# More unused matmuls in an attention kernel's opening, and one more unit whose exponentials are added on VectorE

## The chip, the cores and the metric

The kernel runs on one core of a Trainium2 chip. The metric is device time in microseconds (us) of one execution of the whole program. Engines are named as in the profile: PE (TensorE matmul), PEld (its weight load), DVE (VectorE), ACT (ScalarE), POOL (GpSimd) and SP (SyncE, which issues DMAs).

## What is computed

Attention with normalized queries and keys, followed by a two-layer network with a leaky ReLU:

```python
def rmsnorm(x, g):
    return x / np.sqrt(np.mean(x * x, axis=-1, keepdims=True) + 1e-06) * g

def _attn_ref(q, k, v, g_q, g_k):          # q, k, v: 8 x 12 x 448 x 64, float32
    q_n, k_n = (rmsnorm(q, g_q), rmsnorm(k, g_k))
    scores = (1.0 / np.sqrt(64)) * np.matmul(q_n, k_n.transpose(0, 1, 3, 2))
    scores = scores - np.max(scores, axis=-1, keepdims=True)
    attn = np.exp(scores)
    attn = attn / (np.sum(attn, axis=-1, keepdims=True) + 1e-09)
    return np.matmul(attn, v)

def _moe_ref(x, w_in, w_out):               # x: 3584 x 768, w_in: 768 x 2048, w_out: 2048 x 768
    h = x @ w_in
    g = np.maximum(0.01 * h, h)
    return g @ w_out
```

`x` is the attention's output with the twelve heads of a token side by side.

## The kernel before

**Units.** The 96 heads (8 batches of 12) are worked in 24 units of four heads (`u` from 0 to 23; batch `u // 3`). A unit's scores come in seven steps `t`, one for each group of 64 keys per head. `qk` (line 202, with the matmuls in line 199) writes one step's scores into a PSUM slot of two banks (there are two such slots); `ex` (line 209, instruction in line 218) lets ACT take the exponential of it into the tile `et[t]`, 128x896 in 16 bits. Softmax needs one shift for a unit: `shift_max` (line 225) lets DVE take the maximum of the first step (line 236) and put it on a diagonal (line 238); `shift_mm` (line 243) spreads it over the partitions with a small matmul (line 248 in the loop, line 254 in the opening), and DVE makes the bias `eb` of it (lines 249 and 255 to 257). All exponentials of the unit wait for `eb`.

**Sums and values.** When unit `u + 1` has begun, PE multiplies the values of unit `u` (`pv_slot`, line 364) and sums its exponentials. In the units called narrow (4 to 22) the sums come from `zcol` (line 299, matmuls in line 307): four matmuls of 32 columns for each tile of a list that `z_tiles` (line 294) gives. The list is all seven `et[t]`, or, for a unit named in the table `ADDED`, the last ones and one tile `ea` that holds the sum of the first `ADDED[u]`. DVE makes `ea` in `add_e` (line 288, instructions in line 292), with one addition fewer than there are tiles in it. ACT then takes the reciprocal by a logarithm and an exponential (`zcol_ln`, `zcol_inv`), and four DMAs on SP's queue spread it into `rz` (line 334). ACT copies the values' product to `x32` (line 319), and `xmul_sb` on DVE or `xmul_pool` on POOL multiplies both into the network's input `xt` (line 344).

**The network.** Each batch's first layer is 16 groups of six matmuls (`moe1`, line 386) with the ReLU on ACT (line 380); the second layer is taken for pairs of batches, partly by a product with seven multiplications instead of eight (`seven`), for which DVE makes sums of blocks (lines 449 to 458) and puts the results together (line 475). These pieces wait in `queue` with a cost each, and `fill` (line 726) takes as many of them as fall due after each of a unit's four stages `d` (stage 0 has step 0, stages 1 to 3 have two steps each). After each piece one of the `jobs` of the stage is called; what is left of the jobs comes at the end of the stage. The order in which instructions are written is the order in which each engine works: the schedule is made by hand.

**The loop around unit 7.** In stage 2 of a unit that has four or more added tiles, `add_e(u)` and then `xmul_sb(u - 1)` are called directly after the exponentials, ahead of the jobs. In units 6 and 7 before, which have no entry in `ADDED`, `xmul_sb(u - 1)` is the last job of stage 2, behind the normalization of unit `u + 2` (`prep_rinv` on ACT, `prep_norm` in line 171 on DVE, and a transposing DMA, `prep_trd`).

**The opening.** Units 0 to 2 are written out step by step (lines 769 to 949). For unit 0, `prep_norm` makes normalized q and k in 16 bits, in chunks; PE transposes them (`tr`, line 801), ACT and DVE copy the result into `qkT` (lines 752, 756, 758), and the scores follow. `warm(n, bank)` (line 764) issues `n` matmuls of a 128x128 tile of ones with itself, into columns of a bank that nobody reads. Before there are eight such places: 32 and 42 ahead of unit 0's transposes, then 6, 12, 8, 10, 8 and 12 in the opening of units 0 to 2. The single banks come from a ring of four (`aux`).

Of the kernel before, what the change touches and what calls it, by code (L numbers as in the profile page):

```python
# [18 lines left out]
def kernel(  # L19
# [37 lines left out]
    def aux(shape, dtype, name):  # L57
        if held:
            return held[0].pop(0)
        return psum.tile(shape, dtype, tag="aux", bufs=4, name=name)  # L60
# [51 lines left out]
    st = {}  # L112
# [25 lines left out]
    def buf(u, name):  # L138
        if name not in st[u]:
            shape, dtype, bufs = SHAPES[name]  # L140
            st[u][name] = prep_p.tile(shape, dtype, tag=name[:2] if bufs == 3 and name != "qkT" else name, bufs=bufs, name=name)
        return st[u][name]
# [3 lines left out]
    def prep_sq(u, c=ALL, tis=BOTH):  # L146
        for ti in tis:
            nc.scalar.activation(buf(u, f"sq{ti}")[:, :, c[0]:c[1]], raw[u][ti][:, :, c[0]:c[1]], AF.Square)  # L148
# [44 lines left out]
    def slot():  # L193
        return psum.tile([P, 2, 512], FP32, tag="sT", bufs=2, name="sT")

    def score(u, t, banks):
        for r in range(2):
            for a in range(2):
                nc.tensor.matmul(banks[a][64 * r:64 * r + 64, 0:S].rearrange("p (t x) -> p t x", t=NS),  # L199
                                 kT(u, r, a, t), qT(u, r, a), start=True, stop=True)  # L200

    def qk(u, steps):
        st[u]["sT"] = []
        for t in steps:
            sT = slot()
            score(u, t, (sT[:, 0], sT[:, 1]))
            st[u]["sT"].append((t, sT))

    def ex(u):
        s = st[u]  # L210
        if "et" not in s:
            s["et"] = epool.tile([P, NS, 2, S], FP16, tag="et", name="et")
        for t, sT in s["sT"]:
            if isinstance(sT, list):
                for a in range(2):
                    nc.scalar.activation(s["et"][:, t, a], sT[a][:, 0:S], AF.Exp, bias=s["eb"], scale=1.0)
            else:
                nc.scalar.activation(s["et"][:, t], sT[:, :, 0:S], AF.Exp, bias=s["eb"], scale=1.0)  # L218
# [21 lines left out]
    def shift_bank(u):  # L240
        st[u]["pb"] = aux([P, 512], FP32, "pb")
# [39 lines left out]
                                     e[64 * r:64 * r + 64, a], start=(i == 0), stop=(i == len(ets) - 1))  # L281

    HS = S // 2
    ADDED = {u: 4 for u in (10, 11, 13, 16, 17, 19)}
    ADDED.update({3: 5, 4: 5, NU - 1: 5})
    ADDED.update({u: 3 for u in (8, 14, 20, 22)})

    def add_e(u):
        s = st[u]
        s["ea"] = zpool.tile([P, 2, S], FP16, tag="ea", name="ea")  # L290
        for t in range(1, ADDED[u]):
            nc.vector.tensor_tensor(s["ea"], s["et"][:, 0] if t == 1 else s["ea"], s["et"][:, t], op=ALU.add)  # L292

    def z_tiles(u):
        s = st[u]
        ets = [s["et"][:, t] for t in range(NS)]
        return ets[ADDED[u]:] + [s["ea"]] if "ea" in s else ets

# [465 lines left out]
    def warm(n, bank):  # L764
        for x in range(n):
            nc.tensor.matmul(bank[:, P:2 * P], onesp, onesp, start=True, stop=True)

    with tc.manual_schedule():
# [7 lines left out]
        wbank = aux([P, 512], FP32, "warm")  # L776
# [1 line left out]
        for a in range(2):  # L778
            nc.vector.scalar_tensor_tensor(gdup[:, a], grow[:, 0], 0.125, grow[:, 1], op0=ALU.mult, op1=ALU.mult)
        nc.tensor.matmul(gps[:, 0:1], gdup.rearrange("o a d -> o (a d)"), one32, start=True, stop=True)  # L780
        warm(42, wbank)
        prep_sq(0, CA, (0,))
        prep_sq(0, CB, (0,))
        prep_sq(0, ALL, (1,))
# [11 lines left out]
        def tr(u, ti, chunks, tp=None):  # L796
            if tp is None:
                tp = aux([P, NS, P], FP16, "tp")
            for c, copy in chunks:
                for x in range(*c):  # L800
                    nc.tensor.transpose(tp[:, x, :], buf(u, "n16")[:, ti, x].rearrange("p a d -> p (a d)"), ident16)
                copy(buf(u, "qkT")[:, ti, c[0]:c[1]], tp[:, c[0]:c[1]], ti == 0)
            return tp

        tr(0, 0, ((CA, acopy),))
        tr(0, 0, ((CB, acopy),))
        tpk = tr(0, 1, ((K0, vcopy),))
        prep_sq(1, ALL, (0,))
        qk(0, STEPS[0])
        shift_max(0)  # L810
# [7 lines left out]
        load_v(1)  # L818
        load_v(2)
        shift_bank(0)  # L820
        warm(6, st[0]["pb"])
        shift_mm(0)
        prep_ssq(1)

# [56 lines left out]
        for f in range(2):  # L881
            load_w_out(8 * f, 8)
        qk(1, (2,))
        ex(1)
        trn(2, 0, vcopy)
        qk(1, (3,))
# [27 lines left out]
        prep_sqp(5)  # L914
        load_v(5)
        qk(2, (2,))
        ex(2)
        trn(3, 0, vcopy)
        trn(3, 1, vcopy)
# [31 lines left out]
        for u in range(3, NU):  # L951
            for d in range(4):
                if d > 0 or u > 3:
                    qk(u, STEPS[d])
                    if d == 0:
                        shift_max(u)
                        if u == 6:
                            xmul_sb(u - 2)
                        if narrow(u - 1):
                            pv_slot(u - 1)  # L960
                            zcol(u - 1)
                            shift_mm(u)
                            pv_out(u - 1)
                        else:
                            zsum_slot(u - 1)
                            pv(u - 1)
                            shift_mm(u)
                            zinv(u - 1)
                    ex(u)
                    if d == 0 and narrow(u - 1):  # L970
                        zcol_ln(u - 1)
                if d == 2 and ADDED.get(u, 0) > 3 and u < NU - 1:
                    add_e(u)
                    if u > 4:
                        xmul_sb(u - 1)
                jobs = []

                def job(fn, *args):
                    jobs.append(lambda: fn(*args))

                if d == 0:
                    if u == 3:
                        prep_norm(4)
                        gate(4)
                    elif narrow(u - 1):
                        if u < NU - 1:
                            job(zcol_inv, u - 1)
                    else:
                        xmul(u - 1)
                    if u + 4 < NU:  # L990
                        job(load, u + 4)
                    if u + 3 < NU:
                        load_v(u + 3)
                    if u < 6:
                        prep_sqp(u + 3)
                if d == 1 and narrow(u - 1) and not 5 <= u < 8 and ADDED.get(u, 0) < 4:
                    xmul_pool(u - 1)
                if u == NU - 1:
                    if d == 1:
                        job(zcol_inv, u - 1)  # L1000
                if fed(u, d) and u > 3:
                    push(u // NQ - 1)
                if (u, d) in ((3, 1), (4, 0)):
                    for ti in range(2):
                        prep_tr(u + 1, ti, VV)
                if d == 1 and 5 <= u < NU - 1:
                    job(prep_g, u + 1)
                if u + 2 < NU:
                    if d == 1:
                        if ADDED.get(u) == 3:  # L1010
                            job(lambda u: (prep_ssq(u + 2), add_e(u)), u)
                        else:
                            for ti in range(2):
                                job(prep_ssq, u + 2, ALL, (ti,))
                    if d == 2:
                        job(prep_rinv, u + 2)
                        for ti in range(2):
                            job(prep_norm, u + 2, ALL, (ti,))
                        if u > 3:
                            job(prep_trd, u + 2)  # L1020
                if d == 1 and 4 <= u < 8:
                    job(weight_sum, u - 4, 0)
                if d == 0 and 5 <= u < 9:
                    job(weight_sum, u - 5, 1)
                if d == 2 and 6 <= u < 8:
                    job(xmul_sb, u - 1)
                if d == 1 and u == NU - 2:
                    jobs.append(lambda: None)
                    job(add_e, u)
                if u == NU - 2 and d == 0:  # L1030
                    for n, tile_ in ((1, (raws, "rq", 3)), (2, (raws, "rk", 3)), (3, None), (4, (prep_p, "sq", 3))):
                        job(win_sum, n, 1, tile_)
                    for n in (3, 1, 2, 4):
                        job(x_sum, LATE, n)
                if u == NU - 1 and d == 3:
                    job(add_e, u)
                    job(xmul_sb, u - 1)
                if d == 3 and 6 <= u < NU - 3:
                    for ti in range(2):
                        job(prep_sq, u + 3, ALL, (ti,))  # L1040
                fill(u, d, jobs)
# [39 lines left out]
```

## Time and profile before

| what | value |
|---|---|
| median of four timed runs | 418.12 us (418.05 to 418.16) |
| profiled execution, its own time | 417.42 us |
| its span, first to last instruction | 415.6 us |
| mean granted TensorE clock in it | 0.999 |
| PE busy | 398.5 us, 96% of the span |
| DVE busy | 302.0 us, 73% |
| ACT busy | 303.6 us, 73% |
| POOL busy | 68.8 us, 17% |
| DMA | 62.41 MB, mean 150 GB/s |

How to read it: times are from the span's start. A row of the timeline gives the start, the time until the last of the row's instructions ends, engine, line, operation, what is written from what with its shape, and how many instructions; the bracket is the engine's idle time before it and who ended it. The chain view is the work that ended last, followed backwards: at each step what released the instruction, or the one before it on its engine. Matmuls overlap: one alone takes longer than the distance from one to the next in a row of them. The page's second part has one digit for each fortieth of the span, the busy share in tenths.

### The profile page before, as it was taken

What the parts mean: (1) busy time and instruction counts of PE and PEld (TensorE: products, weight loads), DVE (VectorE), ACT (ScalarE), POOL (GpSimd) and SP (SyncE); (2) the same over time, 40 slices, a digit from 0 to 9 for tenths busy, and PEclk for the clock granted to TensorE, in tenths of its full rate; (3) what the DMA queues carried; (4) which work ended last, traced back from release to release, by engine and by line L of the source; (5) the groups of instructions that cost most, each with busy time, mean ns of one, the idle gap of its engine ahead of it and who ended that gap; (6) DMA issues with size and microseconds to landing.
All of it is one profiled execution on the core that took longest, in us unless ns stands there. A gap on an engine that the chain in (4) does not pass through costs nothing.

```text
span 415.6 us, 9315 instructions
## 1 busy us (share of the span) xinstructions
PE 398.5 (96%) x3807; PEld 218.6 (53%) x3807; DVE 302.0 (73%) x485; ACT 303.6 (73%) x474; POOL 68.8 (17%) x70
## 2 busy tenths in 40 slices
PE   8787999999999999999999999999999999999995
PEld 7454444544445544455445544455445557558863
DVE  5888897986688756866668756867669788557762
ACT  6998888678887699867987689867985657653600
POOL 1867432200010200020020100020002202000000
PEclk9999999999999999999999999999999999999999
DMA  6999998889666995678664996788552460033023
GB/s 212 264 258 250 240 247 160 200 162 208 148 155 88 219 241 101 152 180 176 155 156 70 221 204 127 147 175 183 158 99 45 121 158 9 9 76 77 2 56 97
DMA packets 71950, 62.41 MB, mean 150 GB/s; under 512 B 36324, under 2 KB 67044, under 8 KB 71908
## 3 DMA queue, kind: packets, MB, share of 16 engines
q1 hardware_dynamic: 61312, 49.62, 47.8%
q0 software_dynamic: 10272, 11.80, 18.1%
q8 instruction: 30, 0.49, 0.5%
q10 hardware_dynamic: 324, 0.39, 0.3%
q14 instruction: 12, 0.10, 0.1%
HBM read 45.61 MB, written 11.01 MB: 136 GB/s over the span
## 4 chain that ended last, share of the span: by engine, by line
PE 78%; DVE 9%; ACT 8%; issue 3%; DMA 1%; SPq 0%; DVEq 0%; ACTq 0%
PE hps L386 27%; PE sT L199 8%; PE sT L364 5%; PE ma L468 5%; PE md L468 5%; ACT et L218 5%; PE mc L468 5%; PE bank L588 4%; PE bank L468 4%; PE op L427 4%; PE mb L468 2%; DVE n L171 2%; PE zc L307 2%; PE sT L468 2%; DVE sT L236 1%
## 5 line engine op out<-in xcount | busy, mean ns | idle before, releaser
L218 ACT ACTIVATE et<-sT,eb 128x896 f16<-128x896 f32 x166 | 159.5, 1011 | 18.8 <-PE sT L199 17.0
L386 PE MATMUL hps<-xt,win 128*128 128x448 f16 x600 | 120.8, 353 | 0.2 <-DVE xt L373 0.2
L386 PEld LDWEIGHTS <-win 128*128 128x128 f16 x612 | 56.8, 98 | 58.1 <-issue 9.7
L380 ACT ACTIVATE gt<-hps 128x448 f16<-128x448 f32 x100 | 54.0, 556 | 6.1 <-PE hps L386 5.3
L199 PE MATMUL sT<-qkT 64*64 64x448 f16 x664 | 52.4, 363 | 4.4 <-ACT et L218 3.4
L159 DVE TENSOR_REDUCE ssq<-sq 128x14 f32<-128x896 f32 (+2 forms) x49 | 50.1, 1058 | 0.4 <-ACT sq L148 0.4
L468 PEld LDWEIGHTS <-sa 128*128 128x128 f16 x352 | 32.8, 98 | 26.3 <-issue 6.1
L128 POOL DMA_DIRECT2D vt<-in_v_dram x24 | 17.9, 748 | 173.1 <-PE sT L364 166.4
L319 ACT COPY x<-sT 128x896 f32<-128x896 f32 x19 | 17.2, 907 | 34.1 <-DVE sT L249 34.1
L199 PEld LDWEIGHTS <-qkT 64*64 64x64 f16 x672 | 15.4, 104 | 37.8 <-issue 33.6
L468 PEld LDWEIGHTS <-gt 128*128 128x128 f16 x264 | 25.2, 98 | 19.0 <-issue 2.5
L171 DVE TENSOR_TENSOR n<-rq,rinv 128x896 f16<-128x896 f32 (+2 forms) x25 | 26.2, 1050 | 9.5 <-ACT rinv L165 9.5
L344 POOL TENSOR_TENSOR xt<-x,rz 128x896 f16<-128x896 f32 x9 | 19.1, 2119 | 79.3 <-DMA rz<-zs 71.0
L364 PE MATMUL sT<-et,vt 64*64 64x448 f16 x532 | 28.5, 349 | 0.3
L427 PE MATMUL op<-wout,gt 128*128 128x384 f16 x160 | 28.4, 326 | 0.0
L236 DVE TENSOR_REDUCE sT<-sT 128x1 f32<-128x896 f32 x22 | 24.1, 1094 | 4.7 <-PE sT L199 4.5
L292 DVE TENSOR_TENSOR ea<-ea,et 128x896 f16<-128x896 f16 x25 | 15.6, 626 | 15.6 <-ACT et L218 14.8
L364 PEld LDWEIGHTS <-vt 64*64 64x64 f16 x672 | 20.7, 107 | 11.3 <-issue 1.7
L171 DVE TENSOR_TENSOR n<-rk,rinv 128x896 f16<-128x896 f32 (+2 forms) x26 | 26.1, 1012 | 0.0
L427 PEld LDWEIGHTS <-gt 128*128 128x128 f16 x192 | 17.6, 98 | 14.3 <-issue 3.0
L468 PE MATMUL ma<-wout,gt 128*128 128x384 f16 x128 | 23.5, 326 | 0.0
L292 DVE TENSOR_TENSOR ea<-et 128x896 f16<-128x896 f16 x13 | 8.8, 677 | 11.8 <-ACT et L218 11.8
(143 smaller groups left out, 544.3 us busy)
## 6 DMA issues: line engine op xcount, KB each, us to landing
rq<-in_q_dram SPq DMA_DIRECT2D x24, 448.0 KB, 4.2
rk<-in_k_dram SPq DMA_DIRECT2D x24, 448.0 KB, 5.7
out_dram<-ost SPq DMA_DIRECT2D x52, 192.0 KB, 3.0
rz<-zs SPq DMA_DIRECT2D x76, 112.0 KB, 2.3
vt<-in_v_dram POOLq DMA_DIRECT2D x24, 224.0 KB, 5.3
win<-in_moe_w_in_dram POOLq DMA_DIRECT2D x8, 384.0 KB, 14.0
wout<-in_moe_w_out_dram POOLq DMA_DIRECT2D x2, 1536.0 KB, 28.3
out_dram<-ost SPq DMA_DIRECT2D x4, 96.0 KB, 2.1
```

What stands on the lines that cost most here:

```text
L159: nc.vector.tensor_reduce(buf(u, "ssq")[:, ti, :, c[0]:c[1]], buf(u, f"sq{ti}")[:, :, c[0]:c[1]], axis=AXL.X, op=ALU.add)
L171: nc.vector.tensor_tensor(buf(u, "n16")[:, ti, c[0]:c[1]].rearrange("p s a d -> p a s d"), src[:, :, c[0]:c[1]], buf(u, "rinv")[:, ti, :, ...
L199: nc.tensor.matmul(banks[a][64 * r:64 * r + 64, 0:S].rearrange("p (t x) -> p t x", t=NS), kT(u, r, a, t), qT(u, r, a), start=True, stop=True)
L218: nc.scalar.activation(s["et"][:, t], sT[:, :, 0:S], AF.Exp, bias=s["eb"], scale=1.0)
L236: nc.vector.tensor_reduce(s["spare"][:, 511:512], sT[:, :, 0:S], axis=AXL.XY, op=ALU.max)
L292: nc.vector.tensor_tensor(s["ea"], s["et"][:, 0] if t == 1 else s["ea"], s["et"][:, t], op=ALU.add)
L344: eng.tensor_tensor(xts[b][:, g], s["x32"], s["rz"], op=ALU.mult)
L364: nc.tensor.matmul(s["pv"][r][64 * a:64 * a + 64, 0:S], vts[u % NV][64 * r:64 * r + 64, a, t], s["et"][64 * r:64 * r + 64, t, a], start=(t ...
L380: nc.scalar.activation(dst, src, AF.Prelu, bias=0.0, scale=1.0, alpha=0.01)
L386: nc.tensor.matmul(hps[:, 0:S], win16[:, kt // 2, kt % 2, ts(ft, P)], xt[:, kt // 2, kt % 2], start=(kt == 0), stop=(kt == KT - 1))
L427: nc.tensor.matmul(op2[:, 0:HC], gt[:, ft, ds(col(t), P)], wout16[:, ft, ds(HC * half, HC)], start=(ft == 0), stop=(ft == FT - 1))
L468: nc.tensor.matmul(bank[:, 0:HC], a[:, f], b[:, f], start=(first and f == 0), stop=(f == HF - 1), skip_group_check=not first)
```

## The change

Two things are edited. In the opening, `warm` gets 48 instead of 42 matmuls ahead of unit 0's transposes and 10 instead of 6 ahead of its `shift_mm`, and three new calls of 6, 6 and 12: after the first of unit 0's k transposes, after `qk(1, (2,))` and after `qk(2, (2,))`. They write into banks (`wbank`, and the `pb` of units 1 and 2) that are there already.

Unit 7 gets an entry of 4 in `ADDED`. So in its stage 2 DVE adds its first four exponential tiles (three additions), and `zcol(7)` in unit 8's first stage goes over four tiles in place of seven. By the condition that is there already (line 972) unit 6's multiply is called right behind these additions; the line that made it a job of unit 7 now holds for unit 6 alone.

```diff
-    ADDED = {u: 4 for u in (10, 11, 13, 16, 17, 19)}
+    ADDED = {u: 4 for u in (7, 10, 11, 13, 16, 17, 19)}
...
-        warm(42, wbank)
+        warm(48, wbank)
...
         tpk = tr(0, 1, ((K0, vcopy),))
+        warm(6, wbank)
         prep_sq(1, ALL, (0,))
         qk(0, STEPS[0])
...
-        warm(6, st[0]["pb"])
+        warm(10, st[0]["pb"])
         shift_mm(0)
...
         qk(1, (2,))
+        warm(6, st[1]["pb"])
         ex(1)
...
         qk(2, (2,))
+        warm(12, st[2]["pb"])
         ex(2)
...
-                if d == 2 and 6 <= u < 8:
+                if d == 2 and u == 6:
                     job(xmul_sb, u - 1)
```

## The prediction

> **What bounds the kernel now.** I read the page first, then the chain that ended last, then the order of time around the edited places.
>
> ```profile
> PE   8787999999999999999999999999999999999995
> PEclk9999999999999999999999999999999999999999
> PE 78%; DVE 9%; ACT 8%; issue 3%; DMA 1%; SPq 0%; DVEq 0%; ACTq 0%
> ```
>
> TensorE (PE) is 90% busy or more in 35 of 40 slices. Only the first four slices (about 42 us) and the last have room, and the filler matmuls go into the first four. In order of time the chain shows who sets the end in the opening and who does later:
>
> ```profile
> 7.06 2.22 DVE n L171 x4
> 9.28 0.15 DVE qkT L752
> 9.47 0.41 PE sT L199 x4
> ```
>
> Columns: start, length, what. Up to about 43 us VectorE (DVE) and ScalarE (ACT) hold nearly the whole chain: normalize, transpose, score, maximum, exponential. PE is a short step between them. From 43 us on the chain is PE almost without a break. So a microsecond of PE time is worth nothing in an opening gap, everything on the opening's chain, and nearly everything at unit 7 (95 to 111 us) or 8.
>
> **The clock.** The granted clock reads 1.00 in the thinnest stretches of the opening, and falls only after the last matmul (410.0 to 411.4 us):
>
> ```profile
> 8.50:11.50 3.00, 1.41 (x20) 1.00 1.02 364
> 32.00:35.00 3.00, 1.41 (x26) 1.00 1.11 248
> 415.00:415.60 0.60, 0.00 (x0) 0.63 0.00 0
> ```
>
> Columns: stretch, us, PE busy and instructions, granted clock, DMA share, GB/s. The reading is blind to the very start, so I use spacing too:
>
> ```profile
> 1.16 3.59 PE L766 MATMUL warm<-onesp 128*128 128x128 f16 x32 [1.16 <-DVE onesp L80]
> ...
> 6.31 0.89 PE L766 MATMUL warm<-onesp 128*128 128x128 f16 x13
> ```
>
> One unused matmul takes 0.22 us alone (219 ns is the shortest of line 766), so 32 of them were spaced (3.59 - 0.22)/31 = 109 ns and the later 13 (0.89 - 0.22)/12 = 56 ns. PE starts at half speed and is at full speed before 6.3 us. The opening's transposes keep that spacing (seven in 0.56 at 33.55 and at 34.55: (0.56 - 0.22)/6 = 57 ns), so in the profiled execution there is no slow stretch left for more fillers to remove. Clock term: 0.
>
> The Trainium skill (TensorE: Matmul & The Clock Gate, section "Why this matters for your kernels") says the clock drops back after an idle gap of more than about 3 us. The longest gap that the opening shows is 1.16 us, so by that rule the fillers buy nothing either, and it speaks against this part of the change. The same page, section "A second HAM failure mode: psum-queue depth-cycling", tells of a kernel whose many short idles made the clock go up and down; by that the fillers could buy something, and the sum would be lower by what the first rival below has.
>
> **The fillers, part by part.** 6 + 6 + 4 + 6 + 12 = 34 matmuls of 56 ns.
>
> The six added to the 42 lie on the path.
>
> ```profile
> 7.32 0.55 PE L766 MATMUL warm<-onesp 128*128 128x128 f16 x7
> 7.80 0.28 PE L801 MATMUL tp<-ident,n 128*128 128x128 f16 x2
> ```
>
> The last of the 42 starts at 7.32 + 6 x 0.056 = 7.65, so PE is free at 7.71. The first transpose starts at 7.80, just after the normalized chunk is ready (7.06 + 0.68 = 7.74). Six more hold PE until 7.71 + 0.34 = 8.05, so the first four transposes are 0.25 late. Behind them wait the two ACT copies of q, which run back to back from 8.23 to 9.39 (8.23, 1.16 us, x2); they start 0.25 late and end at 9.64. The first score at 9.47 needs both these copies and the DVE copy that ends at 9.42 and starts it 0.05 later. ACT's release was 9.39 + 0.05 = 9.44, so 0.03 is spare and the score is 0.22 late. The chain goes on from it to the maximum (9.91) and the exponential (12.23), so all that is late by 0.22, and no DMA stands in the chain from 5.05 us on to absorb it. I take **+0.22**; bounds 0 (the chunk comes later in a run and PE waits anyway) and +0.34 (all six count).
>
> The other four groups lie in PE idle time that the rows show: six after the first k transpose in 0.77 us (up to the score at 9.47; 0.34 used); four more before the maximum's matmul at 11.45, idle 0.82 (0.22 used); six after the score at 23.20, idle 0.51 before the transpose at 24.10 (0.34 used); twelve after the score at 32.03, idle 1.16 before 33.55 (0.67 used). All four gaps end by DVE, which these matmuls don't touch; they write unread columns of banks that PE itself writes next. Cost **0**, and 1.57 in all were the cover gone.
>
> **Unit 7.** Three additions of 0.626 us (line 292) are new on DVE, 1.88 us; the multiply of unit 6 (line 344, 1.08 us) goes from behind the two normalizations of unit 9 to ahead of them.
>
> ```profile
> 104.41 1.90 ACT L218 ACTIVATE et<-sT,eb 128x896 f16<-128x896 f32 x2
> 107.24 1.09 DVE L171 TENSOR_TENSOR n<-rq,rinv 128x896 f16<-128x896 f32 x1 [4.98 <-ACT rinv L165]
> 110.04 1.08 DVE L344 TENSOR_TENSOR xt<-x,rz 128x896 f16<-128x896 f32 x1
> 111.72 1.09 DVE L236 TENSOR_REDUCE sT<-sT 128x1 f32<-128x896 f32 x1
> 113.18 0.22 PE L248 MATMUL sT<-dg,onesp 128*128 128x64 f16 x2
> ```
>
> DVE sits idle 4.98 us from 102.26. The first two additions fit there at once (their tiles are ready by 103.46). The third needs tile 3, the first of the two exponentials at 104.41, done at 105.41; it ends near 106.0, the multiply near 107.1, and the normalization at 107.24 was waiting for ACT anyway. Unit 10 has this very order:
>
> ```profile
> 153.71 0.63 DVE L292 TENSOR_TENSOR ea<-ea,et 128x896 f16<-128x896 f16 x1 [1.71 <-ACT et L218]
> 154.26 1.08 DVE L344 TENSOR_TENSOR xt<-x,rz 128x896 f16<-128x896 f32 x1
> ```
>
> and its normalization follows at 155.51, after ACT. So on DVE it costs **0**; without the gap it would be 1.88. The gain is on PE: the sums of unit 7, in unit 8's first step, go from 28 small matmuls to 16. A sum of 16 of the same form, of another unit with four added tiles, stands later in the chain:
>
> ```profile
> 112.46 0.79 PE zc L307 x28
> ...
> 254.64 0.50 PE zc L307 x16
> ```
>
> (start, length, what). The difference gives **-0.29**. The matmul that spreads the maximum follows at 113.18 and needs DVE's maximum (111.72) and diagonal (ending at 113.13). Here the moved multiply decides: without it at 110.04, DVE could start the maximum 1.01 earlier, at 110.71, so the score (110.75 + 0.38 + 0.05 = 111.18) sets it; the diagonal is done at 111.18 + 1.12 + 0.29 = 112.59, and PE gets there at 113.18 - 0.29 = 112.89. PE doesn't wait. Had the multiply stayed, the diagonal would have held the whole gain back. Bounds: -0.34 (the 12 by the spacing 0.79/28) to 0.
>
> The multiply's other side: it waits for the reciprocal's four DMAs, issued from 100.82 (the last at 102.7) and landing 2.3 us after issue, so about 105.0, before 106.0. No DMA is added or moved past another.
>
> **Sum.** The profiled execution took 417.42 (span 415.6 and 1.8 around it): 417.42 + 0.22 - 0.29 = 417.35, a change of -0.07. The four timed runs have their median 0.70 higher, at 418.12; so I forecast 418.12 - 0.07 = **418.05**, with the bounds of the terms 417.78 to 418.46.
>
> **Rivals.**
> (1) *The clock does drop in timed runs.* For it: the 0.70 between the median and a profiled execution without a cold stretch in its opening has no cause in the rows. Half clock adds 53 ns to each 128-column matmul (109 - 56); on the chain's seven transposes at 34.55 that alone is 0.37 and on its ten value matmuls at 36.89 (0.76) about as much again, so one cold stretch could be worth 0.70. Against: four runs within 0.11 us of each other don't look like an event that comes and goes. If it is so and the fillers cure it: 418.12 - 0.70 - 0.07 = 417.35, and 417.13 if also the +0.22 is not paid. I take 417.2.
> (2) *Slower: the multiply blocks DVE in unit 7.* It now stands ahead of the normalizations, four sums of the output blocks (lines 449 to 458) and unit 8's maximum. If the reciprocal lands late, all are late, and PE's matmul at line 248 stands with everything behind it. Spare are 112.89 - 112.59 = 0.30 behind the maximum and 0.13 before the normalization; from a landing later than about 106.4 each microsecond costs one. In the profile before, this landing can't be seen, since the multiply came four microseconds later. At 108, with 1.6 lost: 418.05 + 1.6 = 419.6; at 107.4, 419.1. Against it: unit 10's row shows no idle time before its multiply.
> (3) *Unit 7's gain goes lost later*, in one of PE's own waits on DVE or ACT (0.5 us at line 248 in another unit): 418.12 + 0.22 = 418.34.
>
> **Chances.** Forecast 0.42, (1) 0.31, (2) 0.17, (3) 0.10. What a measurement of this kernel can tell from no change is about 0.2%, 0.84 us: 417.28 to 418.96. Most of (1), 0.30 with the low end of the forecast's unknowns, lies below; all of (2) and a part of (3) that grows beyond its sum, 0.21, above; the rest, 0.49, within. The range that leaves out no more than 0.2 is 417.0 to 419.0; the forecast's own is 417.78 to 418.46.
>
> **What would show it.** In the changed profile: first transposes near 8.05 and first score near 9.69; the other four filler groups with idle time still behind them; three additions and the multiply between 102.5 and 107.3 (plus the shift), with no idle time before the multiply by a DMA; 12 + 4 small sums in 0.50; line 248 following them at once. I am wrong if the first score is not late, if spacing of 109 ns turns up after 6 us in either kernel, or if line 248 waits for line 238 in unit 8.

## The result and the profile after

The changed kernel has a median of 417.24 us over 36 timed runs (416.68 to 418.54), the kernel before 418.09 over 54 (417.35 to 419.64). The ratio is 0.9979, 95% interval 0.9973 to 0.9985: faster by about 0.88 us, a small gain, but one that the interval keeps clear of no change. Two executions of the experiments below, one of the kernel before (mean clock 0.948) and one of a kernel with more fillers (0.755), were far slower than all others and are left out of every median, count and ratio. The profiled execution of the changed kernel is one of its longest: 418.30, span 416.5, mean clock 0.995 (the granted clock, averaged over the span). Its page, with the rows that answer to those of before:

```profile
PE   8888999999999999999999999999999999999995
PEclk9899999999999999999999999999999999999999
PE 80%; ACT 8%; DVE 8%; issue 2%; SPq 1%; DMA 1%; ACTq 0%; DVEq 0%
```

The fillers (the unused matmuls) have made the first slices fuller. But the clock's second digit is an 8. In stretches of 2 us (PE busy and instructions, granted clock, DMA share, GB/s) the place is plain:

```profile
14.00:16.00 2.00, 1.37 (x18) 1.00 1.17 245
16.00:18.00 2.00, 1.79 (x18) 0.70 1.05 162
18.00:20.00 2.00, 2.00 (x19) 0.50 1.09 203
20.00:22.00 2.00, 1.71 (x21) 0.95 1.09 250
```

From 16.8 to 20.2 us PE runs at half speed. Shortly before, from 14 to 16 us, real work and fillers together keep it busy for only 1.37 us. That alone doesn't decide it: in the profile of before PE is busy even less in these 2 us (1.23), and its clock stays at 1.00. The single profile of before had no stretch at half speed at all, and the prediction took that for the rule.

The opening of the changed kernel, in order of time:

```profile
5.20 3.49 PE L766 MATMUL warm<-onesp 128*128 128x128 f16 x48
...
7.44 1.15 DVE L171 TENSOR_TENSOR n<-rq,rinv 128x512 f16<-128x512 f32 x2
...
8.52 0.61 PE L801 MATMUL tp<-ident,n 128*128 128x128 f16 x8
8.95 1.16 ACT L756 ACTIVATE qkT<-tp,gcol 128x512 f16<-128x512 f16 x2 [0.83 <-PE tp L801]
...
10.16 0.38 PE L199 MATMUL sT<-qkT 64*64 64x448 f16 x4 [0.69 <-ACT qkT L756]
```

The 48 take 3.49 us where 42 took 2.68 and the first score starts at 10.16, not 9.47: the row names ACT's copy, which waited for transposes that waited for the fillers. The fillers are only part of the delay: the transposes start 0.72 later than before (8.52 for 7.80), of which 0.39 is the normalized chunk, ready at 7.44 + 0.69 = 8.13 for 7.74, and 0.33 the fillers. Unit 7 and unit 8's first step:

```profile
104.91 0.62 DVE L292 TENSOR_TENSOR ea<-et 128x896 f16<-128x896 f16 x1
105.63 0.62 DVE L292 TENSOR_TENSOR ea<-ea,et 128x896 f16<-128x896 f16 x1
107.17 0.62 DVE L292 TENSOR_TENSOR ea<-ea,et 128x896 f16<-128x896 f16 x1 [0.92 <-ACT et L218]
107.72 1.08 DVE L344 TENSOR_TENSOR xt<-x,rz 128x896 f16<-128x896 f32 x1
108.97 1.09 DVE L171 TENSOR_TENSOR n<-rq,rinv 128x896 f16<-128x896 f32 x1 [0.17 <-ACT rinv L165]
...
112.99 1.10 DVE L236 TENSOR_REDUCE sT<-sT 128x1 f32<-128x896 f32 x1 [0.46 <-PE sT L199]
...
114.62 0.23 PE L248 MATMUL sT<-dg,onesp 128*128 128x64 f16 x2
```

The additions, the multiply and the normalization stand as foretold, all about 1.75 later than the times in the profile of before (0.69 from the first score and 1.06 from the half clock in the opening), with no DMA wait before the multiply; the maximum now waits for the score, and the matmul at line 248 waits for nobody.

**Where the time went.** The starts of the units' first scores (rows of line 199) split the span into pieces that hardly vary. In us, for single profiled executions; the last column is the granted clock of the opening:

| kernel | first score | units 0 to 3 | 8 to 9 | 21 to 22 | clock before 43 us |
|---|---|---|---|---|---|
| before | 9.47 | 29.46 | 16.59 | 16.47 | kept |
| before, another execution | 9.61 | 30.12 | 16.59 | 16.47 | half for 6.8 us |
| changed | 10.16 | 30.52 | 16.30 | 15.92 | half for 3.4 us |
| changed, another execution | 10.18 | 29.46 | 16.30 | 15.92 | kept |

Units 3 to 8 take 71.8 and what follows unit 23's first score takes 63.4 in all of them. So the executions differ in four places: the first score, the clock (0 or 0.7 to 1.1), unit 8's first step (-0.29, as predicted), and a piece that nobody had on the list: between the first scores of units 21 and 22, far from every edit, 0.55 are gone. The first score's +0.7 is not an effect of the change alone. In the other execution of the changed kernel the 48 fillers are done at 7.83 and hold nothing; its first score is late because the load of k ends at 5.77 on the chain, for 5.05 in the profile of before.

**The unforeseen piece.** The first scores of units 21 and 22, in the kernel before and in the changed one:

```profile
317.12 0.38 PE L199 MATMUL sT<-qkT 64*64 64x448 f16 x4
333.59 0.38 PE L199 MATMUL sT<-qkT 64*64 64x448 f16 x4
```

```profile
318.57 0.38 PE L199 MATMUL sT<-qkT 64*64 64x448 f16 x4
334.49 0.38 PE L199 MATMUL sT<-qkT 64*64 64x448 f16 x4
```

In the kernel before, DVE and POOL at unit 21:

```profile
311.90 0.42 DVE L455 TENSOR_TENSOR sa<-gt 128x512 f16<-128x512 f16 x1
312.23 2.30 DVE L458 TENSOR_TENSOR sa<-gt,sa 128x512 f16<-128x512 f16 x1
...
318.46 1.08 DVE L236 TENSOR_REDUCE sT<-sT 128x1 f32<-128x896 f32 x1
```

```profile
311.91 2.34 POOL L344 TENSOR_TENSOR xt<-x,rz 128x896 f16<-128x896 f32 x1 [8.35 <-ACT et L218]
```

```profile
319.92 0.22 PE L248 MATMUL sT<-dg,onesp 128*128 128x64 f16 x2 [0.49 <-DVE dg L238]
```

A block sum that takes 0.42 us elsewhere takes 2.30 and ends at 314.53, 0.28 after POOL's multiply does (314.25). Behind it DVE comes late to the maximum, and PE waits 0.49 for the diagonal. (In the other execution of the kernel before, both block sums take 0.42 us and the normalization behind them takes 2.97 instead of 1.08 beside POOL's multiply; the 16.47 and PE's wait of 0.49 are the same.) In the changed kernel:

```profile
313.34 1.30 DVE L455 TENSOR_TENSOR sa<-gt 128x512 f16<-128x512 f16 x1
314.56 0.41 DVE L458 TENSOR_TENSOR sa<-gt,sa 128x512 f16<-128x512 f16 x1
```

```profile
312.17 2.19 POOL L344 TENSOR_TENSOR xt<-x,rz 128x896 f16<-128x896 f32 x1 [7.16 <-DMA rz<-zs]
```

Everything is 1.44 later here, but POOL's multiply only 0.26: it starts 1.18 earlier against DVE's sums, so DVE's sum, which again ends 0.28 after it, is held for 0.9 us instead of 1.9, and PE's matmul waits for nothing. POOL waits for the four reciprocal DMAs, and those differ. The DMA view of the 7 us around them, before (305 to 312 us) and changed (306 to 313):

```profile
q1 hardware_dynamic: 576, 0.46, 29.7%
q0 software_dynamic: 191, 0.16, 14.8%
q8 instruction: 1, 0.02, 0.8%
...
rz<-zs SPq DMA_DIRECT2D x4, 112.0 KB, 2.9
```

```profile
q1 hardware_dynamic: 576, 0.46, 29.4%
q0 software_dynamic: 252, 0.21, 20.3%
...
rz<-zs SPq DMA_DIRECT2D x4, 112.0 KB, 2.3
```

Columns: queue, packets, MB, share; then the issues with the median us to landing. In the kernel before one packet of the instruction queue lies among them. The view of line 334 gives the shortest, median and longest time to landing, before and changed:

```profile
DMA to landing us min/median/max: 2.3/2.9/3.5
```

```profile
DMA to landing us min/median/max: 2.3/2.3/2.3
```

The row of before names ACT as the end of POOL's wait, but the last of the four, issued at 308.2, landed 3.5 later at 311.7, and the multiply began at 311.91. In the changed kernel it is 309.7 + 2.3 = 312.0, and the multiply began at 312.17.

The page counts 30 such packets of 0.49 MB in all, 16 KB each, and PE has 7,614 instructions: one packet for every 254. If these are PE's own instructions, any edit that changes their number moves all later fetches. The traces fit that. In the kernel before this packet comes when PE has begun 5,806 of its instructions, at 309.5 us; in thirteen traces of the kernels here one comes between PE's 5,775th and 5,807th, although that is at 304.2 us in one of them and at 318.1 us in another.

### The profile page after: what moved, and what is told of

It is laid out like the page before. It is cut to its first block, busy times and chain, and to the rows that moved or that the text cites. A ratio compares the mean times of both kernels' runs of the same rounds, so it can differ in the third digit from the quotient of the medians.

```text
span 416.5 us, 9364 instructions
## 1 busy us (share of the span) xinstructions
PE 401.7 (96%) x3829; PEld 221.2 (53%) x3829; DVE 303.2 (73%) x488; ACT 303.4 (73%) x474; POOL 68.7 (16%) x70
## 4 chain that ended last, share of the span: by engine, by line
PE 80%; ACT 8%; DVE 8%; issue 2%; SPq 1%; DMA 1%; ACTq 0%; DVEq 0%
PE hps L386 25%; PE sT L199 8%; PE sT L364 5%; PE ma L468 5%; PE md L468 5%; PE mc L468 5%; ACT et L218 5%; PE bank L588 4%; PE bank L468 4%; PE op L427 4%; PE mb L468 3%; PE zc L307 2%; DVE n L171 2%; PE warm L766 2%; PE sT L468 2%
## 5 line engine op out<-in xcount | busy, mean ns | idle before, releaser
L292 DVE TENSOR_TENSOR ea<-ea,et 128x896 f16<-128x896 f16 x27 | 16.9, 625 | 16.7 <-ACT et L218 15.7
```

## The experiments

Two theories. **C**: the clock is lowered in the opening in some executions and not in others, and fillers decide how many. **F**: the number of PE instructions decides where the fetches fall. Against them stands my own sum. *Lowered* is an execution with a mean clock under 0.997, and in the others the clock is *kept*; the *gap groups* are the four groups of fillers behind the first transposes (6, 4, 6 and 12 more). For each kernel the table has the runs' median and ratio to the kernel before on the same chip, how many executions had a mean clock under 0.997, and the median span of the others. The first row holds all executions of the kernel before in these series.

| kernel | us | ratio, 95% | clock under 0.997 | span, us |
|---|---|---|---|---|
| before | 418.29 | | 77 of 122 | 416.1 |
| changed, both series | 417.27 | 0.9979 (0.9973 to 0.9985) | 7 of 48 | 415.4 |
| unit 7 alone | 417.33 | 0.9979 (0.9970 to 0.9988) | 7 of 11 | 415.2 |
| fillers alone | 418.44 | 1.0003 (0.9992 to 1.0013) | 2 of 11 | 416.7 |
| gap groups alone | 417.28 | 0.9982 (0.9972 to 0.9993) | 1 of 12 | 415.4 |
| unit 7 and 12 | 418.06 | 0.9992 (0.9980 to 1.0005) | 6 of 12 | 415.5 |
| multiply stays | 417.65 | 0.9987 (0.9976 to 0.9999) | 9 of 12 | 415.6 |
| 48 alone | 418.08 | 0.9996 (0.9986 to 1.0007) | 6 of 11 | 416.1 |
| changed with 42 | 417.36 | 0.9983 (0.9969 to 0.9996) | 1 of 11 | 415.6 |
| no later fillers | 418.77 | 1.0012 (0.9999 to 1.0025) | 12 of 12 | none |
| changed with 42, 18, 14 | 417.05 | 0.9965 (0.9951 to 0.9979) | 1 of 17 | 415.25 |

(The ratio of the changed kernel is of its first series, that of the last row of its second.)

**The kernel before again.**

> The kernel before, unchanged, for the clock and span of each of its executions. Theory C (the clock): the executions of the kernel before differ by a clock that drops for one stretch in the opening in some of them and not in others. A drop of one stretch of about 3.4 us at half speed lowers the mean clock from 1.000 to about 0.996; about a third of the executions should show 0.997 or less, and these should be the long ones (418.7 us and more). Theory L (the loads): the executions differ by when the first q and k land; then the mean clock is 0.998 or more in nearly all of them and the time does not go with it. Either way the ratio to the kernel before is 1.000 within 0.0006.

Measured: 418.27, ratio 1.0006 (0.9997 to 1.0014), 5 of 12 lowered; in all executions of the kernel before, 77 of 122, about twice the third that C expected. The median span of these 77 is 416.5 against 416.1 with the clock kept. So the clock does come and go, but lowered executions aren't simply the long ones, as C also expected: some with a span of 415.8 are among them. The profiled one shows 30.12 us from unit 0 to unit 3, for 29.46 with the clock kept. A lowered clock costs 0.4 in the medians and 0.66 in this trace. The time outside the span varies too: it is about 1.8 us, but over 2.1 in 20 of the 122 executions. Only one other kernel shows that, "unit 7 and 12" (4 of 12); the cause is not shown.

**Unit 7 alone.**

```diff
-    ADDED = {u: 4 for u in (10, 11, 13, 16, 17, 19)}
+    ADDED = {u: 4 for u in (7, 10, 11, 13, 16, 17, 19)}
...
-                if d == 2 and 6 <= u < 8:
+                if d == 2 and u == 6:
```

> Only unit 7's edit: three additions and unit 6's multiply in the gap, none of the fillers. My sum, and theory C as well: -0.29 us, ratio 0.9993, with as many lowered clocks as the kernel before. If unit 7 carried the whole gain: -0.88 us, ratio 0.9979.

Measured: 0.9979, as much as the whole change, with the clock as before (7 of 11). My sum for it fails; its pieces don't: units 8 to 9 take 16.30 (-0.29) and units 21 to 22 take 15.92 (-0.55). The mean span of this kernel is 415.56, that of the whole change 415.55: what the 34 fillers add to unit 7's edit is nothing that these runs can tell from zero.

**The fillers alone, and the gap groups alone.**

```diff
-        warm(42, wbank)
+        warm(48, wbank)
...
+        warm(6, wbank)
...
-        warm(6, st[0]["pb"])
+        warm(10, st[0]["pb"])
...
+        warm(6, st[1]["pb"])
...
+        warm(12, st[2]["pb"])
```

> Only the 34 fillers, unit 7 as before. My sum: +0.22 us, ratio 1.0005. Theory C: the rest of the measured gain, -0.88 + 0.29 = -0.59 us, ratio 0.9986, and clearly fewer executions with a mean clock of 0.997 or less than the kernel before (5 of 36 in the changed kernel). Theory L: 0 to +0.22 us.

> The four groups in the later gaps (6, 4, 6 and 12 matmuls) without the six ahead of the first transposes, unit 7 as before. My sum: 0. Theory C with the four gaps as its cause and +0.22 for the six that are left out: -0.59 - 0.22 = -0.81 us, ratio 0.9981. Theory C with the six as its cause (they make the clock rise in time): about 0, and the clock share of the kernel before.

(The second is the same without the first edit.) Measured: 1.0003 and 0.9982. Both keep the clock (2 of 11 and 1 of 12), so the groups in the gaps do that and not the six. But both ratios are made by the other piece as well. The gap groups alone take 15.92 from unit 21 to 22, without a single edit to unit 7. The fillers alone do too, but lose 0.36 between units 9 and 10 (16.28 for 15.92) and 0.49 between units 18 and 19 (16.81 for 16.32), which no other kernel does. They differ from the gap groups by 12 PE instructions; that these two losses are fetches as well fits F and was not tried by itself. The trace of the fillers alone has the same signs for the second one: an instruction packet at 277.5 us, one of the reciprocal's four DMAs landing after 4.1 us instead of 2.3, and a normalization on DVE of 2.10 us instead of 1.08 beside POOL's late multiply.

**Unit 7 and 12 unused matmuls: the instruction numbers put back.** This run tells F from a real worth of unit 7's edit. Beside unit 7's edit, as above, it has:

```diff
         qk(2, (2,))
+        warm(12, st[2]["pb"])
         ex(2)
```

> Unit 7's edit and 12 unused matmuls in one opening gap (after qk(2, (2,)), idle 1.16 us), nothing else. Unit 7 takes 24 instructions from PE's stream, the 12 put 24 back (weight load and matmul each), so from unit 9 on every PE instruction has the number it has in the kernel before. Theory F (instruction fetch): PE's instructions arrive in pieces of 16 KB, one about every 256 instructions, and in the kernel before one of these lands on the reciprocal's DMAs of unit 20 at 309.5 us and costs 0.54 us; unit 7's edit alone moved it away. With the numbers put back it lands there again: gain only unit 7's own -0.29 us (ratio 0.9993, span 0.29 below the kernel before) plus what the clock gives. Rival: unit 7's edit itself is worth -0.85 us; then the span is again 0.85 below, ratio 0.9979.

Measured: 0.9992 (F: 0.9993). Units 8 to 9 take 16.30, so unit 7's gain is there; units 21 to 22 take 16.47 again, exactly the kernel before's. The rows of unit 21:

```profile
q8 instruction: 1, 0.02, 0.9%
...
rz<-zs SPq DMA_DIRECT2D x4, 112.0 KB, 2.9
```

```profile
312.55 2.30 DVE L458 TENSOR_TENSOR sa<-gt,sa 128x512 f16<-128x512 f16 x1
...
318.78 1.08 DVE L236 TENSOR_REDUCE sT<-sT 128x1 f32<-128x896 f32 x1
```

The packet is back, the landing 2.9 again, the block sum 2.30. Twelve matmuls that write what nobody reads, put into idle time at 32 us, cost 0.55 us at 320. In this trace F is shown. Over the twelve executions it is less plain: their mean span, 415.8, is 0.5 to 0.6 below the kernel before's (416.3 on the same chip, 416.4 in all), between F's 0.29 and the rival's 0.85, and the ratio meets F's partly because four of the twelve have the longer time outside the span. How many executions pay the whole 0.55 stays open.

**The multiply stays.**

```diff
-    ADDED = {u: 4 for u in (10, 11, 13, 16, 17, 19)}
+    ADDED = {u: 4 for u in (7, 10, 11, 13, 16, 17, 19)}
...
-                    if u > 4:
+                    if u > 4 and u != 7:
                         xmul_sb(u - 1)
```

> Unit 7's three additions, but unit 6's multiply stays behind the two normalizations as in the kernel before. My step: DVE's diagonal then holds PE's matmul at line 248, and the 0.29 us of the shorter sums is lost at unit 8 (its first step to unit 9's first step as long as before, 16.59 us); only the moved fetch stays: -0.54 us, ratio 0.9987. Rival: the multiply's place doesn't matter: -0.85 us, 0.9979.

Measured: 0.9987, as expected; units 8 to 9 take 16.58, so the shorter sums bring nothing, and 21 to 22 take 15.92. The rows of unit 8's first step show why:

```profile
113.35 0.27 PE L307 MATMUL zc<-ea,onesr 128*32 128x224 f16 x4
113.84 0.22 PE L248 MATMUL sT<-dg,onesp 128*128 128x64 f16 x2 [0.23 <-DVE dg L238]
```

PE finishes the sums early and then waits for DVE's diagonal. The three additions are worth something only with the multiply in front of the normalizations.

**48 alone, and the changed kernel with 42.**

> Only 48 for 42 ahead of the first transposes. My sum: first score 0.22 us late, all of it kept, ratio 1.0005. Theory C for the six (they raise the clock in time, or keep it up): clearly fewer executions with a mean clock under 0.997 than the kernel before (30 of 47). Theory F: the fetch comes 12 instructions earlier, about 1 us, and still meets the DMAs of unit 20, so nothing is gained there.

> The changed kernel with 42 in place of 48: unit 7 and the four gap groups. Sum of what has been measured: unit 7 -0.29, fetch moved away -0.54, clock -0.25 in the mean, and the +0.2 to +0.3 of the six not paid: -1.1 us, ratio 0.9974, below the changed kernel's 0.9979. If the six are needed for the clock, more executions with a lowered clock than the changed kernel's 5 of 36, and a ratio at or above 0.9979.

Measured: 0.9996 and 0.9983. The six don't keep the clock (6 of 11 lowered with them, 1 of 11 without them in the changed kernel). What they cost is not one number. In the profiled execution of 48 alone the group ran faster and the transposes waited for DVE as before:

```profile
4.75 2.85 PE L766 MATMUL warm<-onesp 128*128 128x128 f16 x48
7.98 0.90 PE L801 MATMUL tp<-ident,n 128*128 128x128 f16 x8 [0.38 <-DVE n L171]
```

Here the clock had risen early enough, and the six cost nothing. In the changed kernel's first profile it rose late, the 48 took 3.49, and they held the transposes until 8.52, 0.39 after the chunk, where in the profile of before the transposes started 0.06 after it. With a late rise the 42 hold them too: in the profiles of "unit 7 and 12" and "multiply stays" the 42 took 3.42 and 3.46, and the first scores came at 10.09 and 10.13. The expectation of 0.9974 for the second kernel missed: its median is not below the changed kernel's. In its profiled execution the load of k landed 0.88 later than in the kernel before's (it ends at 5.93 in the chain, for 5.05), and the first score came at 10.35 with the fillers long done. So loads spread the first score as much as the six do, and 11 runs can't separate 0.2 us; what the six cost in the mean stays open. F's expectation for 48 alone was half right: units 21 to 22 take 16.14, so of 0.55 lost 0.33 came back with a fetch that was 12 instructions earlier.

**No later fillers.**

```diff
-        warm(6, st[0]["pb"])
...
-        warm(12, wb)
...
-        warm(8, wb)
...
-        warm(10, st[1]["pb"])
...
-        warm(8, st[1]["pb"])
...
-        warm(12, st[2]["pb"])
```

> The kernel before without the six groups of unused matmuls behind unit 0's transposes (6, 12, 8, 10, 8 and 12 taken out; the first 32 and 42 stay). Theory C: the clock follows how full PE is over stretches of 3.4 us, real work or not; then nearly every execution has a lowered clock, for several stretches (mean clock 0.990 or less), and its span is longer for that by 1 us or more in spite of the fetch, which moves too. Rival: the fillers don't touch the clock; share and mean as in the kernel before (a half to three quarters under 0.997, mean 0.995).

Measured: all 12 executions lowered, mean clock 0.984, ratio 1.0012. In the trace:

```profile
12.00:14.00 2.00, 0.90 (x9) 0.50 1.01 367
14.00:16.00 2.00, 1.15 (x12) 0.50 1.14 308
16.00:18.00 2.00, 2.00 (x21) 0.50 1.11 178
...
22.00:24.00 2.00, 2.00 (x28) 0.50 1.11 255
```

Half clock for several stretches, 30.76 us from unit 0 to 3: 1.30 more than with the clock kept. The span grew by less than that (0.6 in the mean, where C expected 1 or more), since these 112 instructions fewer also moved the fetch (21 to 22 take 15.92). The fillers' effect on the clock is shown in both directions.

**More fillers where the changed kernel lost the clock.**

```diff
-        warm(48, wbank)
+        warm(42, wbank)
...
-        warm(12, wb)
+        warm(18, wb)
...
-        warm(8, wb)
+        warm(14, wb)
```

> The changed kernel with 42 in place of 48 and more fillers where its lowered execution lost the clock: 18 for 12 and 14 for 8 in the gaps between 12.6 and 15.4 us, where PE waits 0.5 us each for ACT. Theory C: no execution under 0.997. After unit 8 PE's instructions have the numbers of the kernel with the gap groups alone, whose fetch met nothing; so the spans should be 0.85 below the kernel before's undisturbed 416.05 in all executions: 415.2, time 417.0, ratio 0.9972 to 0.9975. Rival: the fillers delay the scores behind them; then 417.4 or more.

> The same kernel as the one with 18 and 14 fillers (42 ahead of the transposes, unit 7 and the four gap groups), for a trace of an undisturbed execution and more of its times. Expected from the theories together: ratio 0.9963 to 0.9975, no mean clock of 0.996 or less from a stretch in the opening; unit 8 to unit 9 shorter by 0.29 us and unit 21 to unit 22 by 0.54 us than in the kernel before; idle time left before the scores behind the added fillers.

> The changed kernel unchanged, beside the others on the same chip: ratio 0.9979 as before, a mean clock under 0.997 in about one of seven executions.

Measured: 0.9963 (0.9944 to 0.9982) with 6 runs, less than the 0.9972 to 0.9975 expected, then 0.9965 (0.9951 to 0.9979) with 11; the changed kernel beside the first gave 0.9982 (0.9973 to 0.9992), 2 of 12 lowered. Of 17 executions one was lowered, at 0.996 (half clock from 10.7 to 14.1); "none" was too much. The median of all is 417.05, the lowest of any kernel here, 0.2 under the changed one's; the intervals of the ratios overlap, so that it beats the kernel before is clear and that it beats the changed one is likely. The expectation that units 8 to 9 and 21 to 22 are shorter by 0.29 and 0.55 held (16.30 and 15.92). The same trace loses 0.24 between units 6 and 7, as no other does; its cause is open.

## Why the prediction was right and wrong

The time lay inside the range of 417.0 to 419.0, 0.81 below the forecast of 418.05 and below the forecast's own bounds of 417.78 to 418.46. The change forecast was -0.07, the measured one about -0.85. The range reached down that far for rival (1), whose mechanism gave only a small part of the gain: that the time fell inside is luck.

**Unit 7, -0.29: right**, to the hundredth (16.59 to 16.30), with its mechanism: the multiply's move decides, as the kernel with the multiply left behind shows.

**"No DMA is added or moved past another": the step that failed.** It is true of the program's own transfers. But the instruction fetches are DMAs too, and each PE instruction added or taken away moves them. That term, -0.55 in the traces, which the prediction had at nothing, is most of the difference. The page had shown the queue with its 30 packets and 0.49 MB, and the 2.30 us block sum at unit 21 stood in the trace of before with a PE wait of 0.49 behind it; I had seen this wait, and used it only as a price in the third rival.

**"Clock term: 0": wrong**, because it was read from one execution that happened to keep its clock. It lowers in 77 of 122 executions of the kernel before and 7 of 48 of the changed one. A lowered execution is 0.46 longer in the mean span in the kernel before and 1.14 in the changed one, so fewer of them save about 0.29 - 0.17 = 0.12 us. The reading of the spacing was right for the execution it was read from. One of the prediction's own signs of being wrong came here: PE at half speed after 6 us, in the changed kernel's profile.

**The six of 48, +0.22, bounds 0 to +0.34: a size that depends on the execution.** 0 in one trace and 0.33 in another, by when the clock rises (the spacing of 109 or 56 ns) and when the chunk is ready. The bounds held for these two, the one value did not.

**The other four filler groups, 0 on the path: right.** With the clock kept, units 0 to 3 take 29.46 with and without them.

**Rivals.** (1) had a true mechanism, which is worth 0.12 of the 0.70 that it was given, and nearly the right number (417.2 for 417.24) by chance: it took the 0.70 between the median and the profiled execution for the price of a lowered clock. That execution was just a short one, at 417.42 beside a lowest of 417.35. The rule of the Trainium skill that stood against the fillers (TensorE: Matmul & The Clock Gate, "Why this matters for your kernels": the clock drops after an idle gap of more than about 3 us) doesn't cover this case: here the clock dropped although PE's longest wait in the opening was 1.2 us in the kernel before and 0.7 in the changed one. Its other section, on many short idles ("A second HAM failure mode: psum-queue depth-cycling"), describes what the runs show: one or two stretches at half clock, of 3.4 or 6.8 us, among waits of PE that are all under 1.5 us. (2) didn't happen: the reciprocal was there before the multiply. (3) didn't happen either: the gain of unit 7 stays to the end.

**The sum, as measured.** -0.29 for unit 7, -0.55 for the fetch (if every execution pays it as the traces do) and -0.12 for the clock make -0.96; the mean span fell by 0.83 (416.38 to 415.55). The remaining +0.13 is not explained by a run; later first scores (the six of 48, and loads that land when they will) are a candidate.

## What to carry to other kernels

Count a kernel's instruction fetches among its DMAs: where one falls on a small transfer that a chain waits for, half a microsecond can come and go with an edit that changes an engine's instruction count, and only a run that keeps the edit and puts the count back tells the edit's worth from it. One profiled execution is one draw of the clock and of the loads: look at the clocks of many before a clock term is set to nothing. Cut the span at events that every unit has (here each unit's first score); most pieces then agree to 0.02 us, and what differs shows its place at once.

## What had not been expected of the hardware

PE's clock was lowered in the changed kernel though PE never waited for longer than 0.7 us in its opening; PE was busy for 1.37 of the 2 us from 14 to 16 by the profile, and the drop came at 16.8, and the lowered stretches seen are 3.4 and 6.8 us long. Where a single 16 KB instruction packet fell among four transfers of 112 KB, one of them landed after 3.5 us instead of 2.3, and after 4.0 in another execution. And a 16-bit block sum of DVE that takes 0.42 us took 2.30 beside a multiply of POOL, and 1.30 beside another, ending 0.28 us after POOL's both times.
